# Moving two transposes of a fused attention and MLP-mixer kernel between TensorE, VectorE and the DMA crossbar

## The chip, the cores and the metric

The kernel runs on one core of one Trainium2 chip. The metric is the device time of one execution in microseconds (us); lower is better. All seven inputs and the output lie in the chip's memory in float32, and the kernel computes in bfloat16 with float32 accumulation.

## The reference

Eight batches, twelve heads, 448 tokens, 64 channels per head. The attention has no softmax; its output, with the heads side by side, is the `x` of a mixer that mixes first over tokens and then over channels.

```python
def _attn_ref(q, k, v):                       # (8, 12, 448, 64) each
    scores = scale * np.matmul(q, k.transpose(0, 1, 3, 2))
    attn = np.maximum(scores, 0.0) ** 2 / S
    return np.matmul(attn, v)

def _moe_ref(x, w_tok1, w_tok2, w_ch1, w_ch2):    # x: (8, 448, 768)
    xt = x.transpose(0, 2, 1)
    h = np.maximum(xt @ w_tok1, 0.0) @ w_tok2     # over tokens, 448 -> 256 -> 448
    u = x + h.transpose(0, 2, 1)
    h2 = np.maximum(u @ w_ch1, 0.0) @ w_ch2       # over channels, 768 -> 1536 -> 768
    return u + h2
```

## The kernel before

The work is cut into 48 pairs of heads, six to a batch; pair `s` belongs to batch `s // 6`. Two heads have 128 channels together, which fill the 128 partitions.

One loop runs over `s` from 0 to 51 and is a software pipeline written out by hand: every instruction goes to its engine's queue in the order of the program, and each engine takes its queue in that order. In one pass, the stages of several pairs stand side by side:

- the loads of pair `s + 3` (`load_pair`, L82 to L104, from the POOL queue), and in some early passes a part of the weights: `load_wt1` in pass 0, `load_wt2` in pass 1, the two halves of `wc1` in passes 3 and 5 (L136), the four quarters of `wc2` in passes 7 to 10 (L143);
- the scores of pair `s` (L195, L209), their relu on ScalarE (L179) and square on VectorE (L185);
- `transposes(s + 1)`, which turn q and k of the next pair channel-major on TensorE (L163) and copy them to SBUF (L173);
- `values(s - 1)`, which multiplies by v (L225, L233) and scales into `xT` (VectorE, L241). `xT[b % 2][:, p, :]` has 128 channels on the partitions and 448 tokens, padded to 512 with zeros, along the row: it is channel-major;
- `x_back(s - 2)`, which turns `xT` token-major with four 128x128 TensorE transposes (L259) and one VectorE copy (L267), into `x_sb`;
- `token1` once every two pairs, in odd passes at the end of the pass: the first token matmul for pairs `s - 3` and `s - 2` (L277), which reads `x_sb`. Call the one for pairs 2i and 2i + 1 number i: number 0 is in pass 3, number 1 in pass 5, number 2 in pass 7;
- `token2` in the following pass (L295), and the residual addition `u = x + h` into `uT_sb`, channel-major (VectorE, L303).

When a batch has all its six pairs through `token2` (first in pass 8), `channel_work` calls `u_back` and puts the channel matmuls of that batch into a Python list, `queue`: 16 units of `channel1` (six matmuls of 128x448 each, L332), and six or eight units of `channel2` (12 matmuls of 128x384 each, L350). `fill(0.25)`, called four times a pass, takes units from this list as long as a credit lasts, and so spreads the channel matmuls over the next six passes. A unit's cost in nanoseconds of TensorE is written beside it. So there is no channel work before pass 8, and what is left after the loop is emptied at the end.

`u_back` turns the six channel blocks of `uT_sb` token-major with six DMA transposes through the crossbar, on the SP queue (L320). `channel2` adds this `u_sb` to its result on VectorE (L358) and stores rows of the output from the SP queue (L369).

PSUM has a ring of three banks, `ps_mm` with the tag `bank`, which `transposes`, `x_back`, `token1`, `token2`, `channel1` and `channel2` share in turn. `x_sb` has two buffers (`mix`, `bufs=2`).

Of the kernel before, what the change touches and what calls it, by code (L numbers as in the profile page):

```python
# [10 lines left out]
BF16 = mybir.dt.bfloat16  # L11
AF = mybir.ActivationFunctionType
ALU = mybir.AluOpType
# [3 lines left out]
def kernel(  # L17
# [11 lines left out]
    nc = tc.nc  # L29
# [6 lines left out]
    NP = H // 2  # L36
# [5 lines left out]
    CC = DM // 128  # L42
    EC = DC // 128
    JC = DT // 128
    SP = 512
    HN = DM // 2
    NT = 2 * S // 128
# [7 lines left out]
    mix = ctx.enter_context(tc.tile_pool(name="mix", bufs=2))  # L55
# [3 lines left out]
    ps_mm = ctx.enter_context(tc.tile_pool(name="ps_mm", bufs=3, space=bass.MemoryType.PSUM))  # L59
# [3 lines left out]
    ident = consts.tile([128, 128], BF16, name="ident")  # L63
    kz = [consts.tile([128, NP, 128], BF16, name=f"kz{i}") for i in range(2)]
    vz = [consts.tile([128, NP, 128], BF16, name=f"vz{i}") for i in range(2)]
    xT = [consts.tile([128, NP, SP], BF16, name=f"xT{i}") for i in range(2)]
# [55 lines left out]
    def load_wt2():  # L122
        nc.gpsimd.dma_start(
            out=wt2_nat, in_=moe_w_tok2.rearrange("(c j) s -> j c s", c=JC)
        )
# [57 lines left out]
    def square():  # L183
        for at, sq in squares:
            nc.vector.tensor_tensor(out=sq, in0=at, in1=at, op=ALU.mult)  # L185
        squares.clear()
# [31 lines left out]
    def values(s):  # L218
        b, p = divmod(s, NP)
        v_raw = raws.pop(s)[2]  # L220
        ps = ps_acc.tile([128, 512], FP32, name="acc_ps")
        for c in range(KB):
            sq = at2.pop((s, c))
            for e in range(2):
                nc.tensor.matmul(  # L225
                    ps[64 * e : 64 * (e + 1), :S],
                    lhsT=v_raw[:, e, c, :],
                    rhs=sq[:, e, :],
                    start=(c == 0),
                    stop=False,  # L230
                    skip_group_check=True,
                )
        nc.tensor.matmul(  # L233
            ps[:, :S],
            lhsT=vz[b % 2][:, p, :],
            rhs=at2.pop((s, KB))[:, 0, :],
            start=False,
            stop=True,
            skip_group_check=True,
        )  # L240
        nc.vector.tensor_scalar(  # L241
            out=xT[b % 2][:, p, :S],
            in0=ps[:, :S],
            scalar1=float(alpha2),
            scalar2=None,
            op0=ALU.mult,
        )


    x_tiles, r1_tiles, uT_tiles = {}, {}, {}  # L250
    PG = 2

    def x_back(s):
        b, p = divmod(s, NP)
        if p % PG == 0:
            x_tiles[s // PG] = mix.tile([128, 4, PG, 128], BF16, name="x_sb")
        ps = ps_mm.tile([128, 1024], BF16, tag="bank", name="x_ps")
        for c in range(4):
            nc.tensor.matmul(  # L259
                ps[:, c * 128 : (c + 1) * 128],  # L260
                lhsT=xT[b % 2][:, p, c * 128 : (c + 1) * 128],
                rhs=ident,
                is_transpose=True,
                start=(c == 0),
                stop=(c == 3),
            )
        nc.vector.tensor_copy(  # L267
            x_tiles[s // PG][:, :, p % PG, :],
            ps[:, :512].rearrange("n (c d) -> n c d", c=4),
        )  # L270

    def token1(i):
        x_sb = x_tiles.pop(i)
        ps = ps_mm.tile([128, JC, PG * 128], FP32, tag="bank", name="t1_ps")
        for j in range(JC):
            for c in range(4):
                nc.tensor.matmul(  # L277
                    ps[:, j, :],
                    lhsT=wt1[:, c, j * 128 : (j + 1) * 128],
                    rhs=x_sb[:, c].rearrange("n g d -> n (g d)"),  # L280
                    start=(c == 0),
                    stop=(c == 3),
                )
        r1 = mix.tile([128, JC, PG * 128], BF16, name="r1_sb")
        nc.scalar.activation(r1, ps, AF.Relu)  # L285
        r1_tiles[i] = r1
# [21 lines left out]
        )  # L308


    r2_tiles, u_tiles, out_tiles = {}, {}, {}

    def u_back(b):
        bb = b // 2
        half = NT // 2
        if b % 2 == 0:
            u_tiles[bb] = mix.tile([128, NP, NT, 128], BF16, name="u_sb")
        t = slice(0, half) if b % 2 == 0 else slice(half, NT)
        for p in range(NP):
            nc.sync.dma_start_transpose(  # L320
                out=u_tiles[bb][:, p, t, :],
                in_=uT_tiles[bb][:, p, t.start * 128 : t.stop * 128],
            )

    def channel1(b, e):
        if b % 2 == 0 and e == 0:
            r2_tiles[b // 2] = mix.tile([128, EC, 2 * S], BF16, name="r2_sb")
        uT, r2 = uT_tiles[b // 2], r2_tiles[b // 2]
        off = (b % 2) * S
        ps = ps_mm.tile([128, 512], FP32, tag="bank", name="m1_ps")  # L330
        for g in range(CC):
            nc.tensor.matmul(  # L332
                ps[:, :S],
                lhsT=wc1[:, g, e * 128 : (e + 1) * 128],
                rhs=uT[:, g, off : off + S],
                start=(g == 0),
                stop=(g == CC - 1),
            )
        nc.scalar.activation(r2[:, e, off : off + S], ps[:, :S], AF.Relu)  # L339

    def channel2(bb, t, half):
        r2 = r2_tiles[bb]
        tok = slice(t * 128, (t + 1) * 128)
        cols = slice(half * HN, (half + 1) * HN)
        if half == 0:
            out_tiles[bb, t] = outp.tile([128, DM], FP32, name="out_sb")
        o = out_tiles[bb, t]
        ps = ps_mm.tile([128, 512], FP32, tag="bank", name="m2_ps")
        for e in range(EC):
            nc.tensor.matmul(  # L350
                ps[:, :HN],
                lhsT=r2[:, e, tok],
                rhs=wc2[:, e, cols],
                start=(e == 0),
                stop=(e == EC - 1),
                skip_group_check=True,
            )
        nc.vector.tensor_tensor(  # L358
            out=o[:, cols].rearrange("n (g d) -> n g d", d=128),
            in0=ps[:, :HN].rearrange("n (g d) -> n g d", d=128),  # L360
            in1=u_tiles[bb][:, half * (CC // 2) : (half + 1) * (CC // 2), t, :],
            op=ALU.add,
        )
        if half == 1:
            lo = t * 128
            while lo < (t + 1) * 128:
                hi = min((t + 1) * 128, (lo // QP + 1) * QP)
                b, c = 2 * bb + lo // S, (lo % S) // QP
                nc.sync.dma_start(  # L369
                    out=out[b].rearrange("(p c) m -> c p m", c=QC)[  # L370
                        c, lo % QP : lo % QP + hi - lo, :
                    ],
                    in_=o[lo - t * 128 : hi - t * 128, :],
                )
                lo = hi
            out_tiles.pop((bb, t))

    queue = []

    def channel_work(b):  # L380
        u_back(b)
        for e in range(EC):
            queue.append((6 * 189, lambda e=e: channel1(b, e)))
        half = NT // 2
        for t in range(half) if b % 2 == 0 else range(half, NT):
            for i in range(2):
                queue.append((12 * 163, lambda t=t, i=i: channel2(b // 2, t, i)))

    NS = B * NP
    RESERVE = 2500.0  # L390
    credit = [-RESERVE]
    per_batch = EC * 6 * 189 + NT * (12 * 163)

    def fill(share):
        if not queue:
# [24 lines left out]
    for s in range(NS + 4):  # L420
        if s < NS:
            scores(s, (0, 1))
        if s + PRE < NS:
            load_pair(s + PRE)
        if s == 0:
            load_wt1()
        if s == 1:
            load_wt2()
        if s == 3:
            order_wt2()  # L430
        if s in (3, 5):
            load_wc1((s - 3) // 2)
        if 7 <= s < 11:
            load_wc2(s - 7)
        fill(0.25)
        if 0 <= s - 2 < NS:
            x_back(s - 2)
        square()
        if 0 <= s - 3 < NS and (s - 3) % PG == PG - 1:
            for i in range(PG):  # L440
                token2(s - 3 - (PG - 1) + i)
            if (s - 3) % NP == NP - 1:
                channel_work((s - 3) // NP)
        fill(0.25)
        if s < NS:
            scores(s, (2,))
        if s + 1 < NS:
            transposes(s + 1)
        if 0 <= s - 1 < NS:
            values(s - 1)  # L450
        if s < NS:
            scores_rest(s)
        square()
        fill(0.25)
        if 0 <= s - 2 < NS and (s - 2) % PG == PG - 1:
            token1((s - 2) // PG)
        fill(0.25)
# [32 lines left out]
```

## Time and profile before

| what | value |
|---|---|
| time, median of 3 runs | 423.76 us (423.21 to 423.96) |
| time of the profiled execution | 423.96 us |
| its span (first to last instruction) | 422.2 us |
| granted TensorE clock, mean | 0.982 |
| TensorE matmul busy | 401.4 us, 95% |
| VectorE busy | 230.8 us, 55% |
| ScalarE busy | 212.2 us, 50% |
| DMA, both queues together | 64% of 16 engines' span, 38.74 MB |

A busy share is an average over the whole span; the stages differ, so the rows by stretch of time say more than the table. In the rows of instructions, "busy, mean ns" counts from an instruction's start to its modelled end, and matmuls overlap, so the step from one matmul to the next is shorter than the mean of one. "Idle before" is the time that an engine stood still just ahead of an instruction, with what released it. A DMA's landing is the time from its issue to its last semaphore update.

### The profile page before, as it was taken

What the parts mean: (1) busy time and instruction counts of PE and PEld (TensorE: products, weight loads), DVE (VectorE), ACT (ScalarE), POOL (GpSimd) and SP (SyncE); (2) the same over time, 40 slices, a digit from 0 to 9 for tenths busy, and PEclk for the clock granted to TensorE, in tenths of its full rate; (3) what the DMA queues carried; (4) which work ended last, traced back from release to release, by engine and by line L of the source; (5) the groups of instructions that cost most, each with busy time, mean ns of one, the idle gap of its engine ahead of it and who ended that gap; (6) DMA issues with size and microseconds to landing.
All of it is one profiled execution on the core that took longest, in us unless ns stands there. A gap on an engine that the chain in (4) does not pass through costs nothing.

```text
span 422.2 us, 7829 instructions
## 1 busy us (share of the span) xinstructions
PE 401.4 (95%) x3177; PEld 209.3 (50%) x3177; DVE 230.8 (55%) x450; ACT 212.2 (50%) x313; POOL 130.8 (31%) x196
## 2 busy tenths in 40 slices
PE   6877799999999999999999999999999999999995
PEld 2333354554455554555545554555545555455553
DVE  3788735566556564476355665465645764543022
ACT  2767576446554456644763455644665347611400
POOL 8993556161233331134111612333311000000000
PEclk8699899999999999999999999999999999999999
DMA  8999999689354894268724874537943332012513
GB/s 75 117 148 172 198 173 189 98 98 148 43 54 70 124 135 54 30 97 130 101 30 68 100 128 81 58 64 104 141 46 35 85 75 57 1 31 86 72 49 103
DMA packets 81989, 38.74 MB, mean 92 GB/s; under 512 B 63840, under 2 KB 78368, under 8 KB 81952
## 3 DMA queue, kind: packets, MB, share of 16 engines
q0 software_dynamic: 54432, 21.70, 45.5%
q1 hardware_dynamic: 27520, 16.52, 18.7%
q8 instruction: 25, 0.41, 0.4%
q14 instruction: 12, 0.10, 0.1%
HBM read 43.38 MB, written 11.01 MB: 129 GB/s over the span
## 4 chain that ended last, share of the span: by engine, by line
PE 83%; DMA 6%; ACT 4%; DVE 3%; issue 2%; POOL 1%; ACTq 0%; POOLq 0%
PE m_ps L350 26%; PE m_ps L332 24%; PE sc_ps L195 7%; PE acc_ps L225 6%; PE qkT_ps L163 6%; PE t_ps L277 4%; ACT at L179 4%; PE acc_ps L233 3%; DMA q_raw<-in_q_dram 3%; PE h_ps L295 3%; DMA wc<-in_moe_w_ch_dram 2%; PE sr_ps L209 2%; DVE out_sb L358 2%; PE x_ps L259 1%; DMA kz<-in_k_dram 1%
## 5 line engine op out<-in xcount | busy, mean ns | idle before, releaser
L179 ACT ACTIVATE at<-sc_ps 128x896 bf16<-128x896 f32 x144 | 125.6, 917 | 72.4 <-PE sc_ps L195 72.4
L332 PE MATMUL m_ps<-uT_sb,wc 128*128 128x448 bf16 x576 | 121.6, 353 | 0.0
L350 PE MATMUL m_ps<-wc,r_sb 128*128 128x384 bf16 x672 | 117.2, 326 | 0.0
L185 DVE TENSOR_TENSOR sq<-at 128x896 bf16<-128x896 bf16 x192 | 100.2, 558 | 4.7 <-ACT at L179 4.6
L94 POOL DMA_DIRECT2D v_raw<-in_v_dram x48 | 34.4, 717 | 181.9 <-PE acc_ps L233 168.9
L350 PEld LDWEIGHTS <-r_sb 128*128 128x128 bf16 x672 | 64.5, 98 | 45.8 <-issue 4.4
L339 ACT ACTIVATE r_sb<-m_ps 128x448 bf16<-128x448 f32 x96 | 52.6, 548 | 55.8 <-PE m_ps L332 55.8
L332 PEld LDWEIGHTS <-wc 128*128 128x128 bf16 x576 | 54.1, 98 | 53.0 <-issue 8.6
L358 DVE TENSOR_TENSOR out_sb<-m_ps,u_sb 128x384 f32<-128x384 f32 x56 | 31.2, 557 | 86.9 <-PE m_ps L350 85.6
L267 DVE COPY x_sb<-x_ps 128x512 bf16<-128x512 bf16 x48 | 20.2, 420 | 63.0 <-PE x_ps L259 63.0
L195 PE MATMUL sc_ps<-qkT 64*128 64x448 bf16 x288 | 45.9, 366 | 5.3 <-DVE qkT L173 2.5
L179 ACT ACTIVATE at<-sr_ps 128x448 bf16<-128x448 f32 x48 | 26.1, 543 | 34.2 <-PE sr_ps L209 34.1
L173 DVE COPY qkT<-qkT_ps 128x960 bf16<-128x960 bf16 x48 | 31.4, 654 | 20.2 <-PE qkT_ps L163 20.0
L225 PE MATMUL acc_ps<-sq,v_raw 128*64 128x448 bf16 x288 | 36.5, 362 | 0.0
L82 POOL DMA_DIRECT2D q_raw<-in_q_dram x48 | 32.9, 685 | 10.9 <-DMA wc<-in_moe_w_ch_dram 9.5
L86 POOL DMA_DIRECT2D k_raw<-in_k_dram x48 | 35.0, 728 | 3.3 <-DMA wc<-in_moe_w_ch_dram 2.5
L241 DVE TENSOR_SCALAR xT<-acc_ps 128x448 bf16<-128x448 f32 x48 | 29.8, 620 | 9.5 <-PE acc_ps L233 9.5
L195 PEld LDWEIGHTS <-qkT 64*128 64x128 bf16 x288 | 11.0, 94 | 39.1 <-issue 29.9
L295 PE MATMUL h_ps<-wt,r_sb 128*128 128x448 bf16 x96 | 25.1, 352 | 3.1 <-ACT r_sb L339 2.5
L285 ACT ACTIVATE r_sb<-t_ps 128x512 bf16<-128x512 f32 x24 | 14.3, 597 | 27.1 <-PE t_ps L277 27.1
L303 DVE TENSOR_TENSOR uT_sb<-h_ps,xT 128x448 bf16<-128x448 f32 x48 | 27.5, 614 | 0.0
L277 PE MATMUL t_ps<-x_sb,wt 128*128 128x256 bf16 x192 | 24.9, 273 | 1.0 <-DVE x_sb L267 1.0
(36 smaller groups left out, 234.8 us busy)
## 6 DMA issues: line engine op xcount, KB each, us to landing
q_raw<-in_q_dram POOLq DMA_DIRECT2D x48, 112.0 KB, 3.5
k_raw<-in_k_dram POOLq DMA_DIRECT2D x48, 96.0 KB, 3.6
v_raw<-in_v_dram POOLq DMA_DIRECT2D x48, 96.0 KB, 3.1
out_dram<-out_sb SPq DMA_DIRECT2D x8, 336.0 KB, 2.8
wc<-in_moe_w_ch_dram POOLq DMA_DIRECT2D x2, 1152.0 KB, 13.0
wc<-in_moe_w_ch_dram POOLq DMA_DIRECT2D x4, 576.0 KB, 9.4
out_dram<-out_sb SPq DMA_DIRECT2D x8, 288.0 KB, 2.7
out_dram<-out_sb SPq DMA_DIRECT2D x8, 240.0 KB, 2.7
```

Source lines behind the costliest of these rows:

```text
L86: nc.gpsimd.dma_start(out=k_raw.rearrange("p h c d -> p h (c d)"), in_=k[b, h0 : h0 + 2, :KM].rearrange("h (p c) d -> p h (c d)", c=KB),)
L94: nc.gpsimd.dma_start(out=v_raw.rearrange("p h c d -> p h (c d)"), in_=v[b, h0 : h0 + 2, :KM].rearrange("h (p c) d -> p h (c d)", c=KB),)
L179: nc.scalar.activation(at, ps[:, :, :S], AF.Relu)
L185: nc.vector.tensor_tensor(out=sq, in0=at, in1=at, op=ALU.mult)
L195: nc.tensor.matmul(ps[:, e, :S], lhsT=sb[h, KO + c * 128 : KO + (c + 1) * 128], rhs=sb[h, :S], start=True, stop=True,)
L225: nc.tensor.matmul(ps[64 * e : 64 * (e + 1), :S], lhsT=v_raw[:, e, c, :], rhs=sq[:, e, :], start=(c == 0), stop=False, skip_group_check=True,)
L277: nc.tensor.matmul(ps[:, j, :], lhsT=wt1[:, c, j * 128 : (j + 1) * 128], rhs=x_sb[:, c].rearrange("n g d -> n (g d)"), start=(c == 0), sto ...
L295: nc.tensor.matmul(ps[:, :S], lhsT=r1[:, j, (p % PG) * 128 : (p % PG + 1) * 128], rhs=wt2[:, j, :], start=(j == 0), stop=(j == JC - 1),)
L332: nc.tensor.matmul(ps[:, :S], lhsT=wc1[:, g, e * 128 : (e + 1) * 128], rhs=uT[:, g, off : off + S], start=(g == 0), stop=(g == CC - 1),)
L339: nc.scalar.activation(r2[:, e, off : off + S], ps[:, :S], AF.Relu)
L350: nc.tensor.matmul(ps[:, :HN], lhsT=r2[:, e, tok], rhs=wc2[:, e, cols], start=(e == 0), stop=(e == EC - 1), skip_group_check=True,)
L358: nc.vector.tensor_tensor(out=o[:, cols].rearrange("n (g d) -> n g d", d=128), in0=ps[:, :HN].rearrange("n (g d) -> n g d", d=128), in1=u_ ...
```

## The change

`x_back` becomes one DMA transpose through the crossbar, on the SP queue, of the 128x512 of a pair's `xT`. It is called one pass earlier, straight after `values` of the same pair, and `x_sb` gets another layout. `u_back` and `u_sb` go. In their place `channel2` issues, after its first matmul, three 128x128 matmuls against the identity that add `u` (out of the channel-major `uT_sb`) to the accumulator, and VectorE copies the sum out instead of adding. The planner's cost of a `channel2` unit rises by 3 x 56.

```diff
     def x_back(s):
         b, p = divmod(s, NP)
         if p % PG == 0:
-            x_tiles[s // PG] = mix.tile([128, 4, PG, 128], BF16, name="x_sb")
-        ps = ps_mm.tile([128, 1024], BF16, tag="bank", name="x_ps")
-        for c in range(4):
-            nc.tensor.matmul(
-                ps[:, c * 128 : (c + 1) * 128],
-                lhsT=xT[b % 2][:, p, c * 128 : (c + 1) * 128],
-                rhs=ident,
-                is_transpose=True,
...
-        nc.vector.tensor_copy(
-            x_tiles[s // PG][:, :, p % PG, :],
-            ps[:, :512].rearrange("n (c d) -> n c d", c=4),
+            x_tiles[s // PG] = mix.tile([128, PG, 4, 128], BF16, name="x_sb")
+        nc.sync.dma_start_transpose(
+            out=x_tiles[s // PG][:, p % PG], in_=xT[b % 2][:, p, :]
         )
...
-                    rhs=x_sb[:, c].rearrange("n g d -> n (g d)"),
+                    rhs=x_sb[:, :, c, :],
...
-    def u_back(b):
...
-        for p in range(NP):
-            nc.sync.dma_start_transpose(
-                out=u_tiles[bb][:, p, t, :],
-                in_=uT_tiles[bb][:, p, t.start * 128 : t.stop * 128],
-            )
...
     def channel2(bb, t, half):
...
+            if e == 0:
+                for g in range(CC // 2):
+                    nc.tensor.matmul(
+                        ps[:, g * 128 : (g + 1) * 128],
+                        lhsT=uT[:, half * (CC // 2) + g, tok],
+                        rhs=ident,
+                        start=False,
+                        stop=False,
+                        skip_group_check=True,
+                    )
-        nc.vector.tensor_tensor(
-            out=o[:, cols].rearrange("n (g d) -> n g d", d=128),
-            in0=ps[:, :HN].rearrange("n (g d) -> n g d", d=128),
-            in1=u_tiles[bb][:, half * (CC // 2) : (half + 1) * (CC // 2), t, :],
-            op=ALU.add,
-        )
+        nc.vector.tensor_copy(o[:, cols], ps[:, :HN])
...
     def channel_work(b):
-        u_back(b)
...
-                queue.append((12 * 163, lambda t=t, i=i: channel2(b // 2, t, i)))
+                queue.append((12 * 163 + 3 * 56, lambda t=t, i=i: channel2(b // 2, t, i)))
...
-        if 0 <= s - 2 < NS:
-            x_back(s - 2)
         square()
...
         if 0 <= s - 1 < NS:
             values(s - 1)
+            x_back(s - 1)
```

## The prediction

> **What bounds the kernel now.** I read the first two parts of the page, then the busy time by stretch, then the two halves apart.
>
> ```profile
> span 422.2 us, 7829 instructions
> ...
> PE   6877799999999999999999999999999999999995
> ...
> DMA  8999999689354894268724874537943332012513
> ```
>
> Each digit is 10.6 us. TensorE is full from about 60 us on; before that it is not, and there the DMA engines are. The table of busy time by stretch (PE, PEld, DVE, ACT, POOL, then granted clock, DMA share and GB/s) gives the late part in one row:
>
> ```profile
> 100.00:400.00 300.00, 297.33 (x2334) 156.34 (x2332) 162.94 (x315) 154.29 (x233) 68.64 (x101) 1.00 0.52 77
> ```
>
> TensorE works 297.3 of 300 us, VectorE 163. So after 60 us only TensorE's own work counts, and a delay that exists at 60 us is carried to the end: TensorE's waits after that are seven of 0.36 us (L295), nothing that could swallow it. Before 60 us the chain of waits (start, us, what) shows another bound:
>
> ```profile
> 26.58 9.57 DMA wc<-in_moe_w_ch_dram
> ...
> 36.44 12.70 DMA q_raw<-in_q_dram
> ...
> 49.18 1.08 PE qkT_ps L163 x16
> ```
>
> The first half of `wc1` and then q of pair 9 behind it: `transposes(9)` in pass 8 cannot start before 49.13 us. What stands before that on TensorE may be late by a few us for nothing; beyond, each us counts.
>
> **What the Trainium skill says.** (1) "TensorE: Matmul & The Clock Gate", Part 1, gives 55.6 ns from one warm 128-column matmul to the next. The trace agrees: four L259 transposes take 0.40 us on the timeline and one alone 0.22, so 0.18 / 3 = 60 ns with rounding. (2) "DMA: Bandwidth & Descriptors", section "Issuing engines are not separate DMA queues": SP's transfers share the 16 engines with POOL's and interleave. The trace agrees, as the landing times below show. (3) "VectorE: DVE Perf Modes", section "Why PSUM operands drop a tier": an fp32 PSUM operand holds VectorE to its slowest rate, so the plain copy should cost what the addition did, 557 ns; no run so far shows that copy. (4) The same TensorE page says that a TensorE idle for a window of some 3.4 us falls to half clock. The trace agrees: after a wait of 2.38 us, eight L163 transposes at 49.18 took 0.59 us instead of 0.39, with the clock granted at 0.50 from 49 to 50 us.
>
> **The change part by part.**
>
> ```profile
> L259 PE MATMUL x_ps<-ident,xT 128*128 128x128 bf16 x192 | 18.7, 220 | 0.0
> ...
> L267 DVE COPY x_sb<-x_ps 128x512 bf16<-128x512 bf16 x48 | 20.2, 420 | 63.0 <-PE x_ps L259 63.0
> ```
>
> TensorE loses 192 transposes and gains 56 x 3 = 168 identity matmuls of the same size with the same kind of weight load: 192 - 168 = 24 fewer at 56 ns is **-1.3 us**, nearly all on the path, as almost all stand after 60 us. If the new matmuls cost 70 ns in their place inside an accumulation, it is +1.0 us; I take 56, as L259 ran back to back at that step.
>
> VectorE loses 48 x 420 ns = 20.2 us and keeps 56 operations of 557 ns (L358, now copies). That lies under TensorE's work and is worth nothing after 60 us; if the copy were slower, 163 of 300 us busy leaves room. The last copy, at the very end, is on the path at the same 0.56 us. `x_back` no longer takes a bank of the ring; TensorE hardly waits for one now, so zero.
>
> SP issues 48 DMA transposes as before (6 a batch for `u_back`, now 6 a batch for `x_back`), each 4 blocks of 128 tokens, not 3 or 4 (3.5 on average). Its in-order queue also holds the stores L369; a transpose waits behind those whose VectorE operation stands earlier in the program than its own, so it loses only their issue times of some 0.4 us. Stores behind a transpose wait for its issue, 1.3 us, and nobody waits for them soon.
>
> **The new wait** is the part that decides. `token1` now waits for a DMA landing, and behind `token1` in TensorE's queue stands everything: the next scores, and with them ScalarE and VectorE. The room it has is from the `xT` scale (L241) of the second pair to `token1` (L277). On the timeline (start, us, then the instruction):
>
> ```profile
> 31.11 0.61 DVE L241 TENSOR_SCALAR xT<-acc_ps 128x448 bf16<-128x448 f32 x1
> ...
> 34.41 1.04 PE L277 MATMUL t_ps<-x_sb,wt 128*128 128x256 bf16 x8
> ...
> 39.14 0.36 PE L163 MATMUL qkT_ps<-ident,k_raw 128*64 128x128 bf16 x6 [1.46 <-DMA k_raw<-in_k_dram]
> ...
> 40.46 0.62 DVE L241 TENSOR_SCALAR xT<-acc_ps 128x448 bf16<-128x448 f32 x1 [0.20 <-PE acc_ps L233]
> ...
> 43.85 1.04 PE L277 MATMUL t_ps<-x_sb,wt 128*128 128x256 bf16 x8
> ```
>
> The room is 34.41 - 31.72 = 2.7 us for token1 number 1, 43.85 - 41.08 = 2.8 us for number 2. How long a transpose takes to land in that stretch (issues by kind, last figure median us to landing, window 26 to 60 us):
>
> ```profile
> q_raw<-in_q_dram POOLq DMA_DIRECT2D x6, 112.0 KB, 9.8
> ...
> u_sb<-uT_sb SPq DMA_TRANSPOSE x6, 8.5
> ```
>
> All six of batch 0's `u_back`, issued from 30.12 to 49.58 us, took 8.1 to 9.2 us; the 42 later ones 2.3 to 6.4 (median 3.2), with the weights loaded. I take **8.5 us** in this stretch. Step by step:
>
> - Number 0 (25.14 us): its second `x_back` would issue at 21.3; loads issued then took 4.8 to 5.2 us, so it lands near 26.2, 1.0 late. The next scores waited for L173 until 26.72 anyway; with one copy fewer on VectorE, 0.5 us remain.
> - Number 1: issue at 31.7, +0.5 and less a copy of 0.4, so 31.8; lands 40.4 with 0.1 of issue; 6.0 late. TensorE then reached the k transposes of pair 7 at 39.14 - 1.46 = 37.68, 3.3 us later, and waited there until 39.14: now 43.7, so 4.6 of the 6.0 stay.
> - Number 2: L241 ended 1.94 us after those k transposes began: 45.6; with 0.1 and 8.5, the landing is at 54.2 against 43.85.
> - `transposes(9)`: TensorE reached it 2.95 us after token1 number 2 (46.80), then waited to 49.18. Now 54.2 + 2.95 = 57.1, which is **+8.0 us**, and q of pair 9 has long landed.
> - Number 3 had 6.9 us of room (52.52 to 59.39), and loads issued at 58 to 62 us landed in 5 to 6.5; later ones have 6.0 to 8.6 against 2.3 to 6.4, the last one 3.3 (379.10 to 382.40), when loads are over and single landings are near 2.5. I take zero for all these; upper bound 24 x 0.4 = 10 us, if the 6.4 were usual.
>
> Sum: 8.0 - 1.3 = **+6.7 us** against the profiled execution's own 423.96 (its span of 422.2 and 1.8 around it, which stay), so 430.7. The median is 0.2 lower, so 430.5. With a landing of L us, the two waits give 2L - 9.0: at 6.5 us +4.0, at 10 us +11.0. The loads in that stretch took 8 to 16 us, so 10 is possible; the `u_back` transposes no longer compete there, but about as many `x_back` do. Half clock after two waits of over 4 us adds up to 1.5 us; the kernel before pays for one such stretch at 49 us.
>
> **The rivals.**
>
> A: *the landing hides.* `x_back` issues earlier than `u_back` did and in another place of the DMA backlog; with a landing of 5 us the two waits of TensorE for k and q take up all but 2 x 5 - 9.0 = 1.0, and 1.0 - 1.3 is -0.3, 423.5 us; at 4.5 us and below nothing is left but the -1.3: 422.5. It decides below some 5.1 us. For it: later transposes land in 3.2. Against: all six in this stretch needed over 8.
>
> B: *every token1 waits.* If landings exceed 6.0 us in the full stretch too, half of the 24 wait 0.3 to 0.8 us more: 430.5 + 12 x 0.3 to 0.8, so 434 to 440. For it: one landing of 6.4 behind stores and loads. Against: the median of 3.2.
>
> C: *the saving is eaten*: identity matmuls at 70 ns take the -1.3 away: 432.8. Against: L259's step.
>
> That the change doesn't do what it says is excluded: the built program has 24 matmuls fewer and the 48 transposes on SP.
>
> **How the numbers follow.** Main case 0.78 (424.6 to 434); A 0.14, of which 0.09 is faster than 0.2% (0.85 us, about what a measurement of this kernel can tell from no change) and 0.05 within; B and C together 0.08, both slower. Slower 0.86. The range 423.8 to 434.5 leaves out most of A and of B.
>
> **What would show it.** Right: token1 (L266 in the changed kernel) with idle time of 4 to 10 us before it, released by the DMA of `x_sb`, at about 40 and 54 us and none after 60; `transposes(9)` near 57 us; x_sb landings near 8.5 us before 60 us; 168 identity matmuls 56 ns apart; L358's successor at 557 ns. Wrong: `transposes(9)` still at 49 us (A), or idle time before L266 in every second pass (B).

## The result and the profile after

The changed kernel took **438.5 us** (436.92 to 438.98, four runs) against 423.86 us for the kernel before (423.21 to 424.02): the ratio is **1.034**, 95% interval 1.031 to 1.037. The profiled execution took 438.44 us with a span of 435.6, so its span is 13.4 us longer; another 1.1 us lie outside it (2.8 us around the span instead of 1.8). The other three executions have 1.8 to 1.9 us around spans of 435.0 to 437.2, so that 1.1 us belongs to this one execution. An execution more than 1.5% slower than the fastest of its kernel is left out of the times and ratios here. The forecast was 430.5 with a range to 434.5: the direction was right and the size half of what was measured.

The page of the changed kernel, busy tenths in 40 slices of 10.9 us:

```profile
span 435.6 us, 7754 instructions
...
PE   6764758999999999999999999999999999999995
...
PEclk9759689999999999999999999999999999999998
DMA  8999999368933797439844798339734622012023
```

TensorE now fills up only from the eighth slice on, and its clock dips to 5 and 6 tenths in the third and fifth slice, where it had 9 and 8. From there on it is as full as it was, as the row by stretch (PE, PEld, DVE, ACT, POOL busy; granted clock, DMA share, GB/s) says:

```profile
65.00:430.00 365.00, 361.81 (x2851) 192.14 (x2852) 183.25 (x339) 183.89 (x276) 86.08 (x126) 1.00 0.56 81
```

The waits have one new entry on TensorE (us in total, times, longest), and it is the largest TensorE has:

```profile
PE t_ps L266 <- DMA x_sb<-xT: 16.8, 4, 7.2
```

Four waits, all before 77 us, for the landing of a transposed `xT`. On the timeline, with the `xT` scale (L241) that starts a transpose, the `token1` (L266) that needs it, and the transposes of the next pairs (L163):

```profile
28.67 1.86 PE L266 MATMUL t_ps<-x_sb,wt 128*128 128x256 bf16 x8 [2.44 <-DMA x_sb<-xT]
...
35.02 0.63 DVE L241 TENSOR_SCALAR xT<-acc_ps 128x448 bf16<-128x448 f32 x1
...
45.80 1.89 PE L266 MATMUL t_ps<-x_sb,wt 128*128 128x256 bf16 x8 [7.24 <-DMA x_sb<-xT]
...
52.15 0.61 DVE L241 TENSOR_SCALAR xT<-acc_ps 128x448 bf16<-128x448 f32 x1
...
61.12 1.89 PE L266 MATMUL t_ps<-x_sb,wt 128*128 128x256 bf16 x8 [5.44 <-DMA x_sb<-xT]
...
65.21 0.39 PE L163 MATMUL qkT_ps<-ident,q_raw 112*64 112x112 bf16 x8
```

The last row is `transposes(9)`: 65.21 us, where the kernel before had 49.18. That is **+16.0 us**; token1 number 3 adds a wait of 1.72 at 76.75, and the remaining way to the end is 2.7 us shorter than before with that wait in it. The eight matmuls of one `token1` take 1.86 to 1.89 us instead of 1.04 at the first three waits: TensorE is at half clock there (granted 0.50). For number 0 it was so already from 23.39 us, before that wait began at 26.23.

The two new kinds of instruction cost what the old ones did (groups; busy, mean ns):

```profile
L337 PE MATMUL m_ps<-ident,uT_sb 128*128 128x128 bf16 x168 | 18.5, 219 | 0.0
...
L345 DVE COPY out_sb<-m_ps 128x384 f32<-128x384 f32 x56 | 31.2, 556 | 91.3 <-PE m_ps L327 87.0 <-DMA x_sb<-xT 2.2 <-DMA out_dram<-out_sb 1.5
```

219 ns against 220 for an L259 transpose, and in the trace 56 ns from one start to the next. The copy takes 556 ns against 557 for the addition, which settles what was open about the Trainium skill's page "VectorE: DVE Perf Modes" (section "Why PSUM operands drop a tier"): it agrees.

What the transposes take to land (minimum, median, maximum, from the view of tile `x_sb`; first those issued from 25 to 70 us, then those from 70 to 340 us):

```profile
DMA to landing us min/median/max: 4.9/8.6/11.8
```

```profile
DMA to landing us min/median/max: 3.5/4.2/6.1
```

### The profile page after: what moved, and what is told of

It reads as the page before. It is cut to its first block, busy times and chain, and to the rows that moved or that the text cites. A ratio compares the mean times of both kernels' runs of the same rounds, so it can differ in the third digit from the quotient of the medians.

```text
span 435.6 us, 7754 instructions
## 1 busy us (share of the span) xinstructions
PE 403.7 (93%) x3153; PEld 208.8 (48%) x3153; DVE 215.3 (49%) x402; ACT 212.5 (49%) x313; POOL 130.8 (30%) x196
## 4 chain that ended last, share of the span: by engine, by line
PE 80%; DMA 9%; ACT 5%; DVE 2%; issue 2%; POOL 1%; ACTq 0%; DVEq 0%; POOLq 0%
PE m_ps L327 25%; PE m_ps L309 23%; DMA x_sb<-xT 8%; PE sc_ps L195 7%; PE t_ps L266 6%; PE acc_ps L225 5%; PE qkT_ps L163 5%; ACT at L179 4%; PE h_ps L284 3%; PE acc_ps L233 3%; PE m_ps L337 2%; PE sr_ps L209 2%; DVE qkT L173 1%; DVE uT_sb L292 1%; ACT r_sb L316 1%
## 5 line engine op out<-in xcount | busy, mean ns | idle before, releaser
L185 DVE TENSOR_TENSOR sq<-at 128x896 bf16<-128x896 bf16 x192 | 102.8, 561 | 86.2 <-ACT at L179 86.0
L327 PE MATMUL m_ps<-wc,r_sb 128*128 128x384 bf16 x672 | 126.0, 326 | 0.0
L309 PE MATMUL m_ps<-uT_sb,wc 128*128 128x448 bf16 x576 | 118.6, 353 | 1.5 <-ACT r_sb L316 1.4
L327 PEld LDWEIGHTS <-r_sb 128*128 128x128 bf16 x672 | 63.4, 98 | 40.1 <-issue 4.4
L345 DVE COPY out_sb<-m_ps 128x384 f32<-128x384 f32 x56 | 31.2, 556 | 91.3 <-PE m_ps L327 87.0
L195 PE MATMUL sc_ps<-qkT 64*128 64x448 bf16 x288 | 46.8, 372 | 5.4 <-ACT at L179 4.3
L173 DVE COPY qkT<-qkT_ps 128x960 bf16<-128x960 bf16 x48 | 31.3, 653 | 26.3 <-PE qkT_ps L163 25.7
L266 PE MATMUL t_ps<-x_sb,wt 128*128 128x256 bf16 x192 | 27.4, 290 | 16.8 <-DMA x_sb<-xT 16.8
L82 POOL DMA_DIRECT2D q_raw<-in_q_dram x48 | 32.8, 683 | 10.2 <-DMA wc<-in_moe_w_ch_dram 9.2
L241 DVE TENSOR_SCALAR xT<-acc_ps 128x448 bf16<-128x448 f32 x48 | 29.8, 620 | 7.9 <-PE acc_ps L233 7.9
L266 PEld LDWEIGHTS <-wt 128*128 128x128 bf16 x192 | 19.5, 103 | 24.7 <-DMA x_sb<-xT 13.6
L284 PE MATMUL h_ps<-wt,r_sb 128*128 128x448 bf16 x96 | 23.9, 374 | 0.0
```

Source lines behind the costliest of these rows:

```text
L173: nc.vector.tensor_copy(sb, ps[:, : KO + KM + 128])
L195: nc.tensor.matmul(ps[:, e, :S], lhsT=sb[h, KO + c * 128 : KO + (c + 1) * 128], rhs=sb[h, :S], start=True, stop=True,)
L266: nc.tensor.matmul(ps[:, j, :], lhsT=wt1[:, c, j * 128 : (j + 1) * 128], rhs=x_sb[:, :, c, :], start=(c == 0), stop=(c == 3),)
L284: nc.tensor.matmul(ps[:, :S], lhsT=r1[:, j, (p % PG) * 128 : (p % PG + 1) * 128], rhs=wt2[:, j, :], start=(j == 0), stop=(j == JC - 1),)
L309: nc.tensor.matmul(ps[:, :S], lhsT=wc1[:, g, e * 128 : (e + 1) * 128], rhs=uT[:, g, off : off + S], start=(g == 0), stop=(g == CC - 1),)
L327: nc.tensor.matmul(ps[:, :HN], lhsT=r2[:, e, tok], rhs=wc2[:, e, cols], start=(e == 0), stop=(e == EC - 1), skip_group_check=True,)
```

## The experiments

**Theory 1**: the loss is TensorE waiting for late landings while the loads fill the DMA engines, with what trails behind each wait. **Rivals**: the identity matmuls are dear; the transposes slow the loads and the waits are a symptom; the loss is spread over the whole span.

### Each part alone

`x_back` by DMA alone (against the kernel before; the body of `x_back` is that of the change, `u_back` and the VectorE addition stay):

```diff
-        if 0 <= s - 2 < NS:
-            x_back(s - 2)
...
             values(s - 1)
+            x_back(s - 1)
```

> The first part alone: x_back by DMA transpose in its new place, u_back and the VectorE addition kept as before. Theory 1 (the loss comes from token1 waiting for the landing of x_sb while the weights are being loaded): all the loss is here and TensorE has 192 x 56 ns = 10.8 us less to do, so 423.9 + 14.6 - 9.4 (the 168 identity matmuls of the whole change that are missing here) = 429, with waits before token1 of about 2, 7, 5 and 2 us for numbers 0 to 3. Rival (the loss comes from the identity matmuls, which would cost far more than 56 ns each inside the accumulation): 423.9 - 10.8 = 413.

Measured: 440.92 us, ratio 1.040 (1.034 to 1.046). The loss is in this part, as theory 1 says, but 12 us more of it than worked out. Its profiled execution took 447.2 us, the longest of four, so I read only the pattern of it: beside waits of 4.6, 6.7, 3.8 and 5.9 us at numbers 0 to 3 there are three at token1 numbers 6, 12 and 18 (3.46, 2.25 and 2.52 us). At each of these three, `x_back` stands on SP behind six issues of `u_back`. The whole change does not have this, since it takes `u_back` away; so part two repairs some of what part one breaks.

The residual by identity matmuls alone (against the changed kernel; the body of `x_back` is again that of the kernel before):

```diff
+        if 0 <= s - 2 < NS:
+            x_back(s - 2)
...
             values(s - 1)
-            x_back(s - 1)
```

> The second part alone: residual by identity matmuls, no u_back; x_back on TensorE as before. Theory 1: no waits before token1, and 168 x 56 ns = 9.4 us more on TensorE, so 423.9 + 9.4 = 433.3. Rival (identity matmuls dearer, or they disturb what stands around them): 435 or more. Rival (they hide in gaps): 424.

Measured: 427.96 us, ratio 1.011 (1.009 to 1.013): neither dear nor hidden, but 5 us cheaper than 433.3. A part of that is on the timeline, at `transposes(9)`:

```profile
45.77 0.39 PE L163 MATMUL qkT_ps<-ident,q_raw 112*64 112x112 bf16 x8
```

45.77 us without a wait, against 49.18 after a wait for q: 3.4 us. In the kernel before, the six transposes of batch 0's `u_back` ran in that stretch; with them gone, q of pair 9 lands in time. And no clock dip follows there, which before lasted 3.4 us at half clock, worth up to 1.7. From `transposes(9)` to the end the kernel takes 380.0 us against 373.0, so 7.0 more; 9.4 - 1.7 = 7.7 was to be expected. The rest, 0.7, I can't place.

### Ten pairs back on TensorE

```diff
+    N_PE = 10
...
+        if s >= N_PE:
+            nc.sync.dma_start_transpose(
+                out=x_tiles[s // PG][:, p % PG], in_=xT[b % 2][:, p, :]
+            )
+            return
+        ps = ps_mm.tile([128, 1024], BF16, tag="bank", name="x_ps")
+        for c in range(4):
+            nc.tensor.matmul(
...
+        if 0 <= s - 2 < min(NS, N_PE):
+            x_back(s - 2)
...
-            x_back(s - 1)
+            if s - 1 >= N_PE:
+                x_back(s - 1)
```

> The whole change, but the first 10 of 48 pairs keep the TensorE transposes, so no DMA transpose of x_back is issued before the weights are loaded. Theory 1: no waits before token1; TensorE loses 152 transposes and gains 168 identity matmuls, 16 x 56 ns = 0.9 us more, so 424.8. Rival (the loss is spread over the whole span, or lies in the late part): about 434 to 437.

Measured: 418.04 us, ratio 0.988 (0.986 to 0.990). Ten of 48 pairs make the difference between 438.5 and 418.0, so the whole loss, and more, hangs on the DMA transposes of the first ten pairs; the rival of a loss spread over the span is excluded. All 48 pairs have the new layout of `x_sb` here, so the layout isn't the cause either. `transposes(9)` starts at 46.27 us, 18.9 earlier than in the changed kernel. It is also 7 us faster than I expected, mostly because `u_back`'s early transposes are gone here too (2.9 us at `transposes(9)`, up to 1.7 for the clock dip behind it); some 2 us stay unplaced.

### Landings that nobody waits for

```diff
             values(s - 1)
+            bs, pshadow = divmod(s - 1, NP)
+            shadow = mix.tile([128, 4, 128], BF16, name="shadow")
+            nc.sync.dma_start_transpose(out=shadow, in_=xT[bs % 2][:, pshadow, :])
```

> The kernel before, with an added DMA transpose of xT for each pair, issued where the change issues x_back, into a tile that nobody reads. It measures the landings without anybody waiting. Theory 1 with the cause in the weights' traffic: landings of 8 to 10 us for those issued between 27 and 68 us, 4 to 5 later, and a time of 424 to 426. Rival (long landings come about only because waits push the transposes against the loads; the prediction's 8.5 and 4.9 us would hold without them): about 5 us for the transpose of pair 1, 8.5 for pairs 3 and 5, under 6.9 for pair 7.

Landings of those issued from 16 to 25 us, then of those from 25 to 70 us (view of tile `shadow`):

```profile
DMA to landing us min/median/max: 7.6/7.8/8.1
```

```profile
DMA to landing us min/median/max: 7.8/9.3/10.7
```

The landings are late without any wait feeding back. The transpose of pair 1 took 8.1 us (4.9 was the prediction's figure), those of pairs 3, 5 and 7 took 8.1, 8.9 and 7.8. Two runs gave 427.5 and 433.4 us, more than the 424 to 426 expected: the profiled span of 425.8 is 3.6 longer than before, and `transposes(9)` starts at 51.69, 2.5 late, with the loads of k and q holding TensorE. So the rival "transposes slow the loads" is real at that size, beside the waits.

### Room before the landing is needed

```diff
-        if 0 <= s - 3 < NS and (s - 3) % PG == PG - 1:
+        if 0 <= s - 4 < NS and (s - 4) % PG == PG - 1:
...
-        if 0 <= s - 2 < NS and (s - 2) % PG == PG - 1:
-            token1((s - 2) // PG)
+        if 0 <= s - 3 < NS and (s - 3) % PG == PG - 1:
+            token1((s - 3) // PG)
```

The first condition is that of `token2` and `channel_work`.

> The whole change with token1, token2 and channel_work one pass later, so that a landing has a whole pass more (some 4 to 8 us) before token1 needs it; the DMA transposes themselves stay where they are. Theory 1 (the loss is TensorE waiting for landings and what the waits trail behind them): waits of under 2 us in all before token1 and some 3 us for the later start of the channel work and the transposes' share of the DMA engines, so 419 to 425. Rival 2 (the transposes slow the loads, and the waits are a symptom): the loads of q and k would hold TensorE instead, 432 or more.

Measured: 425.12 us, ratio 1.004 (1.002 to 1.005). The landings of the transposes issued from 25 to 70 us are as late as ever:

```profile
DMA to landing us min/median/max: 3.4/8.6/10.0
```

No `token1` waits for one any more, and 13.4 us of 14.6 are gone. The loads of q and k hold TensorE for 0.5 us at most at a time, so rival 2 does not explain the loss. `transposes(9)` is at 49.40 us. The kernel stays 7 us behind the kernel with ten pairs on TensorE: no channel matmul has run by `transposes(10)` at 56.6 us, where that kernel has had 24 of them (5.0 us) by 53.8, and its clock is halved in two stretches (27.7 to 34.5 and 48.1 to 55.0 us).

### The clock

```diff
         x_sb = x_tiles.pop(i)
+        if i < 4:
+            keep = ps_mm.tile([128, 512], FP32, tag="bank", name="warm_ps")
+            for _ in range((5, 26, 20, 5)[i]):
+                nc.tensor.matmul(keep, lhsT=warm[:, :128], rhs=warm, start=True, stop=True)
```

> The whole change, with 5, 26, 20 and 5 dummy matmuls of 512 columns ahead of token1 numbers 0 to 3, into a bank of the ring, that nobody reads: they fill the waits so that the clock is not halved. Theory 1 with half clock as a large part: the landings stay as late, but the work after each wait runs at full clock, 1.5 to 2 us saved at each of the three long waits: 433 to 435. Rival (half clock costs nothing, since ScalarE and the loads set the pace there): 438 to 439.

Busy time and clock from 44 to 51 us, the changed kernel first, then this one:

```profile
44.00:51.00 7.00, 5.20 (x32) 2.11 (x34) 1.65 (x3) 2.53 (x4) 0.76 (x2) 0.52 1.41 174
```

```profile
44.00:51.00 7.00, 4.91 (x46) 2.21 (x47) 4.24 (x8) 4.49 (x7) 2.04 (x3) 1.00 1.35 196
```

Measured: 435.32 us, ratio 1.028 (1.021 to 1.035); its interval touches that of the changed kernel, so the traces must carry this. `transposes(9)` starts at 61.67 instead of 65.21. From token1 number 2 to it, 2.88 us instead of 4.09 (2.95 in the kernel before); from number 1 to the scale of pair 5, 6.12 instead of 6.96; behind number 0, where the clock was still halved, nothing. So 2.0 of the 3.5 us are the clock, less than the 1.5 to 2 us expected at each of three waits. The rest is landings: number 0 starts 1.0 us earlier (its transpose took 6.6 us instead of 7.8), and pair 3 landed in 9.3 us instead of 10.1. Pair 5 landed in 6.6 us instead of 8.3, but that was not used: the dummies ahead of number 2 ran until 2.1 us after the landing, so the time of this run shows less than the clock is worth.

### The channel weights taken out of the traffic

```diff
-    wc1 = wpool.tile([128, CC, DC], BF16, name="wc1")
-    wc2 = wpool.tile([128, EC, DM], BF16, name="wc2")
+    wc1 = wpool.tile([128, CC, 128], BF16, name="wc1")
+    wc2 = wpool.tile([128, 1, DM], BF16, name="wc2")
```

> The whole change with only a twelfth of the channel weights loaded (one 128-column block of w_ch1 and one 128-row block of w_ch2, used in place of all the others; the output is therefore not the reference's), so that the same matmuls run without the weights' traffic. Theory 1 with the weights as the cause of late landings: x_sb lands within 5 us everywhere, waits before token1 of about 2 us each for numbers 1 and 2 and none after, and a time within 3 us of the same cut made in the kernel before. Rival (landings are late because of the q, k and v loads or the transposes' own speed): waits of over 4 us remain.

> The kernel before with the same cut of the channel weights (only a twelfth is loaded, and the output is not the reference's). The stretch before 60 us is then no longer bound by loads: about 4 us faster than before, 419 to 420, from the two waits of TensorE for k and q of 1.46 and 2.38 us; all theories expect this, it is the measure for the other cut kernel.

`token1` in the changed kernel with this cut:

```profile
28.00 1.87 PE L265 MATMUL t_ps<-x_sb,wt 128*128 128x256 bf16 x8 [4.04 <-DMA kz<-in_k_dram]
...
39.90 1.05 PE L265 MATMUL t_ps<-x_sb,wt 128*128 128x256 bf16 x8 [2.10 <-DMA x_sb<-xT]
...
50.66 1.05 PE L265 MATMUL t_ps<-x_sb,wt 128*128 128x256 bf16 x8 [1.24 <-DMA x_sb<-xT]
```

Times 424.22 and 419.15 us, spans 422.2 and 417.3: with the channel weights' traffic gone, the change costs 4.9 us of span instead of 13.4, still more than the 3 us expected. At `transposes(9)` (53.55 and 45.64 us) it is 7.9 us late instead of 16.0. Numbers 1 and 2 wait 2.10 and 1.24 us, near the 2 us expected, and landings from 25 to 70 us have a median of 4.3. So the weights' traffic is about half of the delay at `transposes(9)`, and not the whole cause. Number 0 waits 4.04 us before any channel weight would have been loaded: its transpose, issued at 21.1, took 6.7 us beside loads of q, k, v and the token weights. (The row names a load of `kz`; the landing of `x_sb` was at 27.86 us, 0.14 before `token1`.) My expectation of 5 us everywhere failed there, and for pair 4 (6.6 us).

### A version that beats both

Three kernels keep the first ten pairs on TensorE and use the DMA for `x_back` after that. The first keeps `u_back` and the VectorE addition as they were (against the kernel before):

```diff
+        if s >= N_PE:
+            nc.sync.dma_start_transpose(
...
-        if 0 <= s - 2 < NS:
+        if 0 <= s - 2 < min(NS, N_PE):
             x_back(s - 2)
...
             values(s - 1)
+            if s - 1 >= N_PE:
+                x_back(s - 1)
```

> x_back by DMA transpose from pair 10 on, TensorE transposes before that, and u_back with the VectorE addition as before: six transposes in a row on SP when a batch is done. TensorE has 152 x 56 ns = 8.5 us less. Theory (an x_back that stands behind six u_back issues of 1.2 us on SP lands 5 us or more too late): waits of 2 to 4 us before token1 number 6, 12 and 18, as in the kernel with x_back alone, so 423.7 - 8.5 + 8 to 10 = 423 to 425. Rival (with the early transposes on TensorE nothing waits): 415.

Measured: 433.82 us, ratio 1.020 (1.014 to 1.026), slower than expected by some 9 us. The SP queue around the first burst that delays an `x_back` (start, length from the first issue to the end of the last, then the instruction):

```profile
97.30 8.93 SPq L327 DMA_TRANSPOSE u_sb<-uT_sb  x6
106.32 15.82 SPq L260 DMA_TRANSPOSE x_sb<-xT  x3
```

and its waits:

```profile
PE t_ps L284 <- DMA x_sb<-xT: 14.4, 7, 5.1
```

The waits at numbers 6, 12 and 18 are there as expected (3.56, 5.09, 3.56 us). For the first, `xT` was ready at 100.72 us and its transpose issued at 106.32, behind the six. What I had left out is what trails behind the waits. From number 11 to 13 the kernel needs 40.2 us where the last one below needs 31.1, so a wait of 5.1 costs 9.1; from 5 to 7 and from 17 to 19 it needs 5.1 and 6.9 us more, with waits of 3.6. Half clock lasts 3.4, 6.8 and 3.4 us at the three. It can account for at most half of its length each time; this was not measured apart.

The other two issue `u_back` pair by pair, right after its `token2`, and use identity matmuls only for the first batches (against the changed kernel; `FIRST_U` is 2 in one and 1 in the other):

```diff
                 token2(s - 3 - (PG - 1) + i)
+                if (s - 3) // NP >= FIRST_U:
+                    u_back(*divmod(s - 3 - (PG - 1) + i, NP))
```

> x_back by DMA from pair 10 on; the residual by identity matmuls for batches 0 and 1, and from batch 2 on by DMA transposes of uT_sb that are issued two by two right after their token2, not six in a row, with the VectorE addition. TensorE has 42 x 4 = 126 identity matmuls x 56 ns = 7.1 us less than the kernel with late x_back and identity matmuls everywhere (418.0): 411. If two u_back issues ahead of an x_back still make token1 wait in every second pass: 415 to 420.

> As the kernel with DMA transposes of uT_sb from batch 2 on, but from batch 1 on: 24 identity matmuls fewer, 1.3 us less, 410, if the last weights (landing until 73 us) don't collide with the new transposes near 70 us; if they do, 411 to 414 with a wait before token1 number 4 or 5.

Measured: 412.32 us (ratio 0.972, 0.970 to 0.974) and **410.22 us** (0.967, 0.965 to 0.969), where 411 and 410 were worked out. SP in the second:

```profile
95.68 2.65 SPq L327 DMA_TRANSPOSE u_sb<-uT_sb  x2
98.42 6.39 SPq L260 DMA_TRANSPOSE x_sb<-xT  x2
```

The next `xT` is ready at 97.28 us and its transpose issued at 98.42, so two issues ahead of it cost 1.1 us, not 5.6. That fits into the room: TensorE waits 0.2 us in all for landings of `x_sb`, and its weight loads 0.5.

## Why the prediction was wrong in size

- **What bounds the kernel, and where the loss falls: right.** All waits lie before 77 us; after that TensorE is full, and the delay is carried to the end.
- **Cost of the instructions: right.** 56 ns an identity matmul, 556 ns a copy, both shown. Rival C is out. Rival B is out for the change (no wait after 77 us), rival A is out by the landings.
- **"The new wait": mechanism right, sum half.** The forecast was +8.0 us at `transposes(9)`, measured +16.0. The same chain, step by step (us):

| step | forecast | measured |
|---|---|---|
| token1 number 0 starts | 26.2 | 28.67 |
| scale of pair 3 done | 31.8 | 35.64 |
| number 1 starts | 40.4 | 45.80 |
| k transposes of pair 7 | 43.7 | 50.84 |
| scale of pair 5 done | 45.6 | 52.76 |
| number 2 starts | 54.2 | 61.12 |
| `transposes(9)` | 57.1 | 65.21 |

- **The first failed term, landings (3.8 us).** For number 0 I took the 4.8 to 5.2 us of loads issued at the same moment. But those were loads of a kernel without the new transposes: with them, the q and k loads issued from 19 to 23 us took 5.9 to 6.8 us in the changed kernel and 7.0 to 7.5 in the shadow, and the transpose itself still a little more, 7.8 and 8.1. That made number 0 2.5 us later than forecast. Pair 3 took 10.1 instead of 8.5, which added 1.6; pair 5 took 8.3, which gave 0.2 back.
- **The second failed term, work between the landings (4.3 us).** The forecast has 5.6 us from number 0 to the scale of pair 3, 5.2 from number 1 to the scale of pair 5, and 2.95 from number 2 to `transposes(9)`. They were 7.0, 7.0 and 4.1. Three things went wrong:
  - 1.0 us: I let 0.5 us of number 0's lateness be swallowed by a wait for L173 and took 0.4 off for a copy. Nothing was swallowed, since everything behind number 0 shifts with it: the first step is 6.58 us long in the kernel before.
  - 0.9 us: I read the second step from a trace in which TensorE waited 1.46 us for k in the middle of it. VectorE used that wait for two residual additions (L303), so the way from the k transposes to the scale looked like 1.94 us. Without a wait and at full clock the whole step takes 6.11 us, in the kernel with the residual alone and in that with the dummy matmuls.
  - 2.4 us: half clock. I had priced it at up to 1.5 us and left it out of the sum. The last two steps took 0.85 and 1.2 us more than at full clock, and the dummy matmuls won back just these 2.0 us. The other 0.4, behind number 0, is argued from its `token1` taking 1.86 us instead of 1.04, not shown.
- **Point (4), the clock.** I said that the trace agrees with an idle window of some 3.4 us. It shows that half clock follows a wait, but at a shorter one: the dip of the kernel before began at 48.84 us, 2.04 us after TensorE had stopped. What the traces show of it stands at the end.
- **Number 3: zero forecast, 1.72 us measured.** Shifted by 16 us, its landing took 8.5 us at 68 us, where the last weights were still being loaded. I had used the loads' times of the kernel before at the old place.
- **"About as many `x_back` do": nearly right in sum, by two large effects.** Taking `u_back` out of the early stretch brought `transposes(9)` 3.4 us forward; adding the transposes of `x_back` alone put it back by 2.5. The kernel with both and a pass more of room has it at 49.40 us, 0.2 later than before.
- **The rest:** the way from `transposes(9)` to the end was forecast 1.3 us shorter and was 2.7 shorter, in spite of number 3's wait of 1.7. Up to 1.7 of the difference is the dip at 49 us that the kernel before pays behind `transposes(9)`; 1.4 are not placed.

## What to carry to other kernels

Before a step moves from an engine to a DMA transpose, compare the room between its producer and its reader with landings of transposes in that very stretch, and replay the whole chain: a wait on an in-order engine delays the producer of the next wait. Where a stretch is full of loads, keep the old way there and use the DMA afterwards; 10 pairs of 48 turned 438.5 into 418.0. And on a DMA queue that also serves short deadlines, spread a burst: six issues of 1.2 us in a row cost 5 to 9 us at each of three places; issued two by two, earlier, they left waits of 0.5 us.

## What the runs showed of the hardware

- A 128x512 DMA transpose took 2.4 us to land with no loads in flight (issued after 350 us), about 4.2 beside loads of q, k and v and stores of the output, and mostly 8 to 12 beside the weights as well. Two of them at 17 and 21 us also slowed the q and k loads around them, from about 5 us to 6 or 7.
- Each DMA transpose occupies SP for 1.2 us. That is nothing for one and 8.9 us from first to last for six.
- TensorE was at half clock for 20.5 us between 23 and 65 us in the changed kernel, in stretches of 10.2, 6.8 and 3.4 us, and for 3.4 in the kernel before. In all the traces such a stretch, where a span shows both its ends, lasted a multiple of 3.41 us.
- It took no idle time of that length. The stretch of the kernel before began after 3.41 us in which TensorE was busy for 1.37. The first of the changed kernel, at 23.39 us, began after 3.41 us with 1.57 busy and no pause over 1.2 in them; one in the kernel with the later `token1`, at 48.15, after 3.41 us with 1.67 busy. Counted in windows of 3.41 us from the edges of these stretches, half clock set in after windows that were busy for up to 0.53 of their time, in all 13 traces, and never after a fuller one. Between 0.43 and 0.53 it did not always set in, so the share alone does not decide.
